# Attention for head pairs on the two halves of the array, with unshifted exponentials, in a kernel of routed attention and a feed-forward

## The chip, the cores and the metric

The kernel runs on one core of a Trainium2 chip, in one launch. The metric is the device time of one execution in microseconds. A core has five engines that are named here as the profile names them: PE (TensorE, with PEld for its weight loads), DVE (VectorE), ACT (ScalarE), POOL (GpSimd) and SP, which issues most transfers.

## The reference

Four batches of eight heads, 768 tokens, 64 numbers per head. Each query and each key is given the nearest of 16 centroids of its head, and a query attends to the keys of its own cluster alone. The result, 3072 tokens of 512 numbers, goes through a feed-forward with a hard-swish between two products.

```python
q_assign = np.argmax(np.einsum('bhsd,hcd->bhsc', q_n, c_n), axis=-1)
k_assign = np.argmax(np.einsum('bhsd,hcd->bhsc', k_n, c_n), axis=-1)
mask = q_assign[:, :, :, None] == k_assign[:, :, None, :]
scores = scale * np.matmul(q, k.transpose(0, 1, 3, 2))
scores = np.where(mask, scores, -1000000000.0)
scores = scores - np.max(scores, axis=-1, keepdims=True)
attn = np.exp(scores)
attn = attn / (np.sum(attn, axis=-1, keepdims=True) + 1e-09)
attn_out = np.matmul(attn, v)          # (B, H, S, D), then x = (B*S, H*D)
h = x @ w_in                           # 512 -> 2048
g = h * np.clip(h + 3.0, 0.0, 6.0) / 6.0
out = g @ w_out                        # 2048 -> 512
```

## The kernel before

All products are in float32 but for the turning of the one-hot clusters. One head is worked at a time (`g` of 32), in six steps of 128 queries (`n` of 192). `xqk` holds per head 80 rows: 64 of q and k with the tokens along the columns (`turn`, L198, on TensorE by way of the identity), and 16 of one-hot clusters (`route`, L212, picks the cluster, `route_turn`, L242, turns the one-hots; those of the keys are -2^60 wherever the cluster is not the key's). One product over the 80 rows thus gives masked scores, 128 queries by 768 keys (`softmax`, L259). VectorE takes the negated maximum (L264), ScalarE the exponentials and their sum (L267), VectorE the reciprocal (L269, L270), GpSimd scales the exponentials (L271). `attn_turn` turns them on TensorE, six blocks per step (L286), and ScalarE and VectorE copy them out of PSUM (L289, L291), half each. After three steps `attn_v` multiplies half a head's values with them, `pv` of 64 rows by 384 queries (L302), and VectorE copies it to `xT` (L306), the input of the feed-forward with its 512 numbers along the rows.

The feed-forward of a batch is a list of 56 items (`ffn_items`): per half sequence 16 upward items of four products with 384 columns (L323), then twelve downward ones of four products with 512 columns (L345). The weights come as float64 bits, 32 chunks, loaded (`load_weights`) and taken apart on VectorE and GpSimd (`decode_weights`), one chunk per step from the first step on.

The order is the program's, moved a little by a scheduler that fills waits. What decides when the feed-forward stands is this:

```python
left = per_batch - (n - 3) % per_batch
for _ in range(-(-len(fill) // left) if n < total else 0):
    fill.pop(0)()
```

The list is filled at the step where `(n - 3) % per_batch` is 47, so `left` is 1 there and all 56 items are issued in that step. What prepares the next head (`prep_items`) lies in the steps of the head before. PSUM pools: `psum_s` two pairs of banks for scores, `psum_t` two banks for everything that is turned, `psum_m` two banks for `pv` and the feed-forward.

Of the kernel before, what the change touches and what calls it, by code (L numbers as in the profile page):

```python
# [19 lines left out]
NCH = S // P  # chunks of 128 tokens in a sequence; chunk j holds the tokens p * NCH + j  # L20
NC2 = 2 * NCH  # q chunks, then k chunks
HALF = S // 2
NHC = NCH // 2
NG = B * H
DM = 512
# [12 lines left out]
@with_exitstack  # L38
def kernel(
    ctx: ExitStack,  # L40
    tc: tile.TileContext,
    q: bass.AP,
    k: bass.AP,
    v: bass.AP,
    centroids: bass.AP,
    moe_w_in: bass.AP,
    moe_w_out: bass.AP,
    out: bass.AP,
):
# [36 lines left out]

    def load(g):
# [9 lines left out]
    # The weights come as the bits of float64: (low, high) words, the high one of sign, 11 exponent  # L97
    # bits and 20 fraction bits. |w| = 2^(e - 1023) (1 + high fraction / 2^20 + low / 2^52), rounded
    # once to float32; the exponent is held to float32's range.

    w_in_v = moe_w_in.bitcast(U32).rearrange("(kt p) (f w) -> kt p f w", p=P, w=2)
    w_out_v = moe_w_out.bitcast(U32).rearrange("(ft p) (m w) -> ft p m w", p=P, w=2)
    chunks = [
        (w_in_sb[:, kt, c * WC : (c + 1) * WC], w_in_v[kt][:, c * WC : (c + 1) * WC])
        for c in range(DFF // WC)
        for kt in range(NKT)
    ] + [(w_out_sb[:, ft], w_out_v[ft]) for ft in range(NFT)]
# [6 lines left out]
    def decode_weights(i):  # L114
        if not 0 <= i < len(chunks):
            return
        dst, raw = chunks[i][0], st.pop(("raw", i))
        lo, hi = raw[:, :, 0], raw[:, :, 1]
        ex = decp.tile([P, WC], U32, name="wex")
        fr = decp.tile([P, WC], U32, name="wfr")  # L120
# [21 lines left out]
        nc.vector.scalar_tensor_tensor(  # L142
            out=dst.bitcast(U32), in0=hi, scalar=0x80000000, in1=fr,
            op0=ALU.bitwise_and, op1=ALU.bitwise_or,
        )

# [1 line left out]

# [294 lines left out]
```

## Time and profile before

| | us |
|---|---|
| median of 3 runs | 1671.39 |
| lowest, highest | 1656.84, 1700.23 |
| span of the profiled execution | 1678.6 |
| TensorE busy in it | 1611.4 |
| VectorE, ScalarE, GpSimd busy | 660.1, 397.7, 254.8 |

The span is counted from the first to the last instruction of the profiled execution. Busy time of TensorE counts each product from its start to its modelled end, and products overlap, so that a mean duration is longer than the spacing of a dense row. The mean granted clock of TensorE over the span is 0.940; its two levels are 1.2 and 2.4 GHz, so 0.5 and 1.0.

### The profile page before, as it was taken

To read this page: it belongs to the slowest core of one execution; us is meant where nothing else is said; L and a number is where in the kernel's file an instruction comes from. 1 tells how busy PE (TensorE), PEld (TensorE's weight loads), DVE (VectorE), ACT (ScalarE), POOL (GpSimd) and SP (SyncE) were. 2 spreads that over 40 slices of the span, in tenths; PEclk is the share of its full clock that TensorE was granted. 3 is DMA by queue.
4 is the path that set the end of the run, shared out by engine and by line. 5 is a ranking of instruction groups with operands and counts; after the bars stand their busy time and mean duration, and the time that the engine had idled before them with its cause. 6 is when DMAs were issued, how large, how long until landed. Compare 5 with 4: busy or idle time off the path is not lost.

```text
span 1678.6 us, 15784 instructions
## 1 busy us (share of the span) xinstructions
PE 1611.4 (96%) x6017; PEld 884.1 (53%) x6017; DVE 660.1 (39%) x1478; ACT 397.7 (24%) x803; POOL 254.8 (15%) x311
## 2 busy tenths in 40 slices
PE   6988889999999999999999999999999999999999
PEld 4544445555545555554545555555554555545453
DVE  5677875411135445520104555341112444542020
ACT  2222233310123333320103333231011333322020
POOL 2445541100001111100001211110000111110000
PEclk9778899999999978999999989799999987999999
DMA  4222321000000000000000000000000000000000
GB/s 129 65 90 89 94 73 29 15 7 12 7 14 28 14 25 19 15 15 13 7 13 21 24 19 19 25 15 4 15 7 13 29 15 5 1 1 1 18 1 19
DMA packets 22107, 42.99 MB, mean 26 GB/s; under 512 B 2576, under 2 KB 14864, under 8 KB 22032
## 3 DMA queue, kind: packets, MB, share of 16 engines
q1 hardware_dynamic: 22032, 41.99, 8.0%
q8 instruction: 48, 0.79, 0.2%
q14 instruction: 27, 0.22, 0.0%
HBM read 35.68 MB, written 6.29 MB: 25 GB/s over the span
## 4 chain that ended last, share of the span: by engine, by line
PE 91%; DVE 4%; POOL 2%; ACT 2%; issue 1%; DMA 0%; SPq 0%; POOLq 0%; ACTq 0%
PE ph L323 20%; PE py L345 20%; PE ps L259 17%; PE pv L302 15%; PE pa L286 9%; PE pr L212 5%; PE pqk L198 2%; PE po L242 2%; ACT pT L289 1%; DVE xqk L203 1%; POOL ex L271 1%; DVE xqk L249 1%; DVE nmx L264 1%; POOL wex L132 0%; ACT ex L267 0%
## 5 line engine op out<-in xcount | busy, mean ns | idle before, releaser
L271 POOL TENSOR_SCALAR ex<-ex,rcp 128x768 f32<-128x768 f32 x192 | 183.4, 957 | 1188.7 <-DVE rcp L270 990.4
L259 PE MATMUL ps<-xqk 80*128 80x384 f32 x768 | 350.3, 569 | 14.0 <-DVE xqk L249 13.1
L323 PE MATMUL ph<-xT,w_in_sb 128*128 128x384 f32 x1024 | 333.0, 487 | 0.0
L345 PE MATMUL py<-w_out_sb,gT 128*128 128x512 f32 x768 | 330.9, 592 | 0.0
L302 PE MATMUL pv<-pT,vt 128*64 128x384 f32 x768 | 285.6, 514 | 0.2 <-ACT pT L289 0.2
L323 PEld LDWEIGHTS ph<-xT,w_in_sb 128*128 128x128 f32 x1024 | 193.9, 190 | 137.5 <-issue 4.9
L345 PEld LDWEIGHTS py<-w_out_sb,gT 128*128 128x128 f32 x768 | 145.9, 190 | 182.0 <-issue 179.9
L289 ACT COPY pT<-pa 128x384 f32<-128x384 f32 x192 | 91.9, 479 | 582.5 <-PE pa L286 581.8
L286 PE MATMUL pa<-ident,ex 128*128 128x128 f32 x1152 | 202.1, 305 | 27.7 <-ACT pT L289 19.9
L286 PEld LDWEIGHTS pa<-ident,ex 128*128 128x128 f32 x1152 | 144.7, 153 | 132.5 <-issue 45.2
L264 DVE TENSOR_REDUCE nmx<-ps 128x1 f32<-128x768 f32 x192 | 183.3, 955 | 77.9 <-PE ps L259 77.2
L267 ACT ACTIVATE ex<-ps,nmx 128x768 f32<-128x768 f32 x192 | 173.1, 902 | 59.8 <-DVE nmx L264 51.2
L259 PEld LDWEIGHTS ps<-xqk 80*128 80x128 f32 x768 | 146.2, 220 | 75.8 <-issue 31.6
L330 ACT ACTIVATE t<-ph,half_c 128x384 f32<-128x384 f32 x128 | 74.4, 581 | 445.1 <-PE ph L323 445.1
L332 DVE SCALAR_TENSOR_TENSOR gT<-t,ph 128x384 f32<-128x384 f32 x128 | 71.0, 555 | 256.9 <-ACT t L330 256.9
L302 PEld LDWEIGHTS pv<-pT,vt 128*64 128x64 f32 x768 | 99.3, 141 | 127.5 <-issue 124.9
L351 DVE COPY y<-py 128x512 f32<-128x512 f32 x24 | 16.6, 692 | 309.2 <-PE py L345 309.2
L291 DVE COPY pT<-pa 128x384 f32<-128x384 f32 x192 | 106.1, 553 | 74.9 <-PE pa L286 74.3
L212 PEld LDWEIGHTS pr<-cnT,xqk 64*128 64x128 f32 x768 | 92.5, 196 | 22.9 <-issue 14.9
L212 PE MATMUL pr<-cnT,xqk 64*128 64x16 f32 x768 | 95.7, 266 | 5.1 <-DVE xqk L203 4.5
L306 DVE COPY xT<-pv 64x384 f32<-64x384 f32 x64 | 35.5, 554 | 150.9 <-PE pv L302 150.7
L198 PE MATMUL pqk<-ident,qk 128*64 128x128 f32 x384 | 63.6, 293 | 0.6 <-ACT xqk L201 0.6
(49 smaller groups left out, 572.3 us busy)
## 6 DMA issues: line engine op xcount, KB each, us to landing
raw<-in_moe_w_in_dram SPq DMA_DIRECT2D x16, 512.0 KB, 3.8
raw<-in_moe_w_out_dram SPq DMA_DIRECT2D x16, 512.0 KB, 3.5
qk<-in_q_dram SPq DMA_DIRECT2D x32, 192.0 KB, 2.4
qk<-in_k_dram SPq DMA_DIRECT2D x32, 192.0 KB, 3.7
vt<-in_v_dram SPq DMA_DIRECT2D x32, 192.0 KB, 2.4
out_dram<-y SPq DMA_DIRECT2D x24, 256.0 KB, 2.0
cen<-in_centroids_dram SPq DMA_DIRECT2D x1, 32.0 KB, 1.8
```

The costliest lines, as they stand in the source:

```text
L198: nc.tensor.transpose(out=pt[:, i], in_=qk[:, j // NCH, j % NCH], identity=ident)
L212: nc.tensor.matmul(pr[:, j], lhsT=xqk[0:D, j], rhs=cnT[:, h * C : (h + 1) * C], start=True, stop=True)
L259: nc.tensor.matmul(sc[:, a], lhsT=xqk[:, i], rhs=xqk[:, NCH + a * NHC : NCH + (a + 1) * NHC], start=True, stop=True,)
L264: nc.vector.tensor_reduce(out=nmx, in_=sc, axis=AX.XY, op=ALU.max, negate=True)
L267: nc.scalar.activation(out=ex, in_=sc, func=ACT.Exp, bias=nmx, scale=1.0, accum_out=den)
L271: nc.gpsimd.tensor_scalar(out=ex, in0=ex, scalar1=rcp, scalar2=1.0, op0=ALU.mult, op1=ALU.mult)
L286: nc.tensor.transpose(out=pt[:, i], in_=ex[:, a, i * P : (i + 1) * P], identity=ident)
L289: nc.scalar.copy(out=dst, in_=pt)
L291: nc.vector.tensor_copy(out=dst, in_=pt)
L302: nc.tensor.matmul(pv[r : r + D, 0:HALF], lhsT=vt[:, j], rhs=pT[:, j], start=(j == 0), stop=(j == NCH - 1),)
L323: nc.tensor.matmul(hh, lhsT=w_in_sb[:, kt, f * P : (f + 1) * P], rhs=xT[:, kt, hf * HALF : (hf + 1) * HALF], start=(kt == 0), stop=(kt == ...
L345: nc.tensor.matmul(py, lhsT=st["g", f][:, i * P : (i + 1) * P], rhs=w_out_sb[:, f], start=(f == 0), stop=(f == NFT - 1),)
```

## The change

The old kernel stays as `general_path`. A new `fast_path` runs first and writes the whole output; a flag that it computes decides whether the old path runs behind it. In the fast path:

- Two heads are worked as a pair (`g` of 16). `turn` turns 128 columns, both heads at once, so that `xf` has the first head in rows 0 to 63 and the second in rows 64 to 127. `route` works on both heads with one product per chunk, against centroids that are zero in the other head's rows. The one-hots lie in `ohs`, zero between the two heads' 16 columns, and are turned to bf16 `xm`.
- `scores` gives keys by queries: 128 keys by 384 queries for each head, f32 over 64 rows, and the mask as a second, bf16 product over 64 rows onto the same PSUM. The exponential is taken without a maximum. `attn_v` uses the exponentials as they are, the two heads to the two halves of the columns of `pv`. No exponential is turned.
- GpSimd adds up the exponentials over the key chunks (`acc`), and `divide` sums them over the rows with a product against ones (`pd`), takes reciprocals on VectorE, and multiplies. There VectorE and GpSimd also keep track of sums and reciprocals for the flag.
- The feed-forward items are spread: `left` is 48 at the step that fills the list, and the number of items is rounded down. 32 weight chunks are taken in 60 steps.
- `psum_t` has one buffer, `psum_v` is new, `qkp` has one buffer. `decode_chunk`, `weight_chunks` and `unit_rows` hold the old code of weights and centroids as functions.

```diff
...
+def fast_path(ctx, tc, ok, q, k, v, centroids, moe_w_in, moe_w_out, out):
...
+    qkp = pool("qkp", 1)
+    vp = pool("vp", 2)
+    xp = pool("xp", 2)
...
+    expp = pool("expp", 4)
+    accp = pool("accp", 2)
+    nump = pool("nump", 2)
...
+    psum_s = pool("psum_s", 2, space=PSUM)
+    psum_v = pool("psum_v", 1, space=PSUM)
+    psum_t = pool("psum_t", 1, space=PSUM)
+    psum_m = pool("psum_m", 2, space=PSUM)
...
+    ones = const.tile([P, D], F32, name="ones")
...
+    ohs = [const.tile([P, NC2, P], BF16, name=f"oh{i}") for i in range(2)]
+    good = const.tile([P, HALF], F32, name="good")
+    inverses = const.tile([P, HALF], F32, name="inverses")
...
+    def turn(g, part):
+        if part == 0:
+            st["xf", g] = xp.tile([P, NC2, P], F32, name="xf")
+        qk, xf = st["qk", g], st["xf", g]
+        pt = psum_t.tile([P, NHC, P], F32, name="pqk", tag="t")
+        for i in range(NHC):
+            j = part * NHC + i
+            nc.tensor.transpose(out=pt[:, i], in_=qk[:, j // NCH, j % NCH], identity=ident)
...
+    def route(g):
+        c0, xf = (2 * g) % H * C, st["xf", g]
+        pr = psum_t.tile([P, NC2, 2, C], F32, name="pr", tag="t")
+        for j in range(NC2):
+            nc.tensor.matmul(
+                pr[:, j], lhsT=xf[:, j], rhs=cnT[:, c0 : c0 + 2 * C], start=True, stop=True
+            )
+        shape = [P, 2 * NC2, C]
+        pr = pr.rearrange("p j t c -> p (j t) c")
+        mx = rtp.tile([P, 2 * NC2], F32, name="mx")
...
+        oh = ohs[g % 2].rearrange("p j (t c) -> p j t c", t=2)
+        tie = tie.rearrange("p (j t) c -> p j t c", t=2)
+        first = first.rearrange("p (j t) -> p j t", t=2)
+        for a, op in ((0, ALU.is_equal), (1, ALU.not_equal)):
+            sl = slice(a * NCH, (a + 1) * NCH)
+            nc.vector.tensor_tensor(
+                out=oh[:, sl, :, 0:C], in0=tie[:, sl],
+                in1=first[:, sl].unsqueeze(3).to_broadcast([P, NCH, 2, C]), op=op,
+            )
...
+    def route_turn(g, part):
+        if part == 0:
+            st["xm", g] = xp.tile([P, NC2, P], BF16, name="xm")
+        xm = st["xm", g]
+        po = psum_t.tile([P, 4, P], F32, name="po", tag="t")
+        for i in range(4):
+            j = part * 4 + i
+            nc.tensor.matmul(
+                po[:, i], lhsT=ohs[g % 2][:, j], rhs=(ident_q if j < NCH else ident_k),
+                start=True, stop=True,
+            )
...
+    def scores(n):
+        g, hf, j = where(n)
+        xf, xm = st["xf", g], st["xm", g]
+        qs = slice(hf * NHC, (hf + 1) * NHC)
+        ps = psum_s.tile([P, 2, 512], F32, name="ps")
+        sc = ps[:, :, 0:HALF]
+        for x, first in ((xf, True), (xm, False)):
+            for t in range(2):
+                r = slice(t * D, (t + 1) * D)
+                nc.tensor.matmul(
+                    sc[:, t], lhsT=x[r, NCH + j], rhs=x[r, qs], start=first, stop=not first
+                )
+        ex = expp.tile([P, 2, HALF], F32, name="ex")
+        nc.scalar.activation(out=ex, in_=sc, func=ACT.Exp, scale=SM_SCALE)
+        st["ex", n] = ex
+        if j == 1:
+            acc = st["acc", g, hf] = accp.tile([P, 2, HALF], F32, name="acc")
+            nc.gpsimd.tensor_tensor(out=acc, in0=st["ex", n - 1], in1=ex, op=ALU.add)
+        elif j > 1:
+            acc = st["acc", g, hf]
+            nc.gpsimd.tensor_tensor(out=acc, in0=acc, in1=ex, op=ALU.add)
+        if hf == 1 and j == NCH - 1:
+            st.pop(("xf", g)), st.pop(("xm", g))
+
+    def attn_v(n):
+        g, hf, j = where(n)
+        if j == 0:
+            st["pv"] = psum_v.tile([P, 512], F32, name="pv")
+        pv, vt, ex = st["pv"][:, 0:HALF], st["v", g], st.pop(("ex", n))
+        for t in range(2):
+            nc.tensor.matmul(
+                pv[t * D : (t + 1) * D], lhsT=vt[:, j, t], rhs=ex[:, t],
+                start=(j == 0), stop=(j == NCH - 1),
+            )
+        if j == NCH - 1:
+            num = st["num", g, hf] = nump.tile([P, HALF], F32, name="num")
+            nc.scalar.copy(out=num, in_=pv)
+            if hf == 1:
+                st.pop(("v", g))
+
+    def divide(n):
+        g, hf, _ = where(n)
+        b, kt = divmod(g, NKT)
+        if kt == 0 and hf == 0:
+            st["xT", b] = xtp.tile([P, NKT, S], F32, name="xT")
+        acc, num = st.pop(("acc", g, hf)), st.pop(("num", g, hf))
+        pd = psum_t.tile([P, 512], F32, name="pd", tag="t")
+        pd = pd[:, 0:HALF]
+        for t in range(2):
+            nc.tensor.matmul(
+                pd[t * D : (t + 1) * D], lhsT=ones, rhs=acc[:, t], start=True, stop=True
+            )
+        rcp = nump.tile([P, HALF], F32, name="rcp")
+        nc.vector.reciprocal(out=rcp, in_=pd)
+        nc.vector.tensor_tensor(
+            out=st["xT", b][:, kt, hf * HALF : (hf + 1) * HALF], in0=num, in1=rcp, op=ALU.mult
+        )
+
+        nc.vector.scalar_tensor_tensor(
+            out=good, in0=pd, scalar=BOUND, in1=good, op0=ALU.is_le, op1=ALU.mult
+        )
+        nc.gpsimd.tensor_tensor(out=inverses, in0=inverses, in1=rcp, op=ALU.add)
...
+    def prep_items(g):
+
+        return {
+            0: lambda: turn(g, 0),
+            1: lambda: turn(g, 1),
+            2: lambda: turn(g, 2),
+            3: lambda: turn(g, 3),
+            5: lambda: route(g),
+            7: lambda: route_turn(g, 0),
+            8: lambda: route_turn(g, 1),
+            9: lambda: route_turn(g, 2),
+        }
+
+    fill = []
+    per_pair = 2 * NCH
+    per_batch = NKT * per_pair
+    total = NPAIR * per_pair
...
+    lag_v, lag_d = 2, 4
+    for n in range(total + lag_d):
+        g, r = divmod(n, per_pair)
+        if n < total:
+            if r == 4:
+                load(g + 2, "q", "k")
+                load(g + 1, "v")
+            scores(n)
+        if lag_v <= n < total + lag_v:
+            attn_v(n - lag_v)
+        m = n - lag_d
+        if m >= 0 and m % NCH == NCH - 1:
+            divide(m)
+            if m % per_batch == per_batch - 1:
+                fill += ffn_items(m // per_batch)
+
+        for i in range(n * 8 // 15, (n + 1) * 8 // 15):
+            decode_weights(i - 1)
+            load_weights(i)
+        if g + 1 < NPAIR and r in (items := prep_items(g + 1)):
+            items[r]()
+        left = per_batch - (m + 1) % per_batch
+        for _ in range(len(fill) // left if n < total else 0):
+            fill.pop(0)()
+    for it in fill:
+        it()
+
+    low = smallp.tile([P, 1], F32, name="low")
+    nc.vector.scalar_tensor_tensor(
+        out=good, in0=inverses, scalar=BOUND, in1=good, op0=ALU.is_le, op1=ALU.mult
+    )
+    nc.vector.tensor_reduce(out=low, in_=good, axis=AX.X, op=ALU.min)
+    pl = psum_t.tile([1, P], F32, name="pl", tag="t")
+    nc.tensor.transpose(out=pl, in_=low, identity=ident)
+    every = smallp.tile([1, 1], F32, name="every")
+    nc.vector.tensor_reduce(out=every, in_=pl, axis=AX.X, op=ALU.min)
+    nc.vector.tensor_copy(out=ok, in_=every)
...
+def general_path(ctx, tc, q, k, v, centroids, moe_w_in, moe_w_out, out):
...
+    ins = (q, k, v, centroids, moe_w_in, moe_w_out)
+    flagp = ctx.enter_context(tc.tile_pool(name="flagp", bufs=1))
+    ok = flagp.tile([1, 1], I32, name="ok")
+    with ExitStack() as inner:
+        fast_path(inner, tc, ok, *ins, out)
+    with tc.If(tc.nc.values_load(ok[0:1, 0:1], min_val=0, max_val=1) == 0):
+        with ExitStack() as inner:
+            general_path(inner, tc, *ins, out)
...
```

The order of TensorE's instructions at the end of the first batch, before: one turn of exponentials, the last values of the batch, and the whole feed-forward behind it (L286 turns, L302 values, L323 and L345 feed-forward, L212 routing, L259 scores).

```order
L286 MATMUL pa<-ident,ex 128x128 x6
L302 MATMUL pv<-pT,vt 64x384 x6
L323 MATMUL ph<-xT,w_in_sb 128x384
L212 MATMUL pr<-cnT,xqk 128x16 x12
L323 MATMUL ph<-xT,w_in_sb 128x384 x63
L345 MATMUL py<-w_out_sb,gT 128x512 x48
L323 MATMUL ph<-xT,w_in_sb 128x384 x64
L345 MATMUL py<-w_out_sb,gT 128x512 x48
L259 MATMUL ps<-xqk 128x384 x2
```

The same engine in the changed kernel, a step of the second batch: scores (L300) of both heads, the mask of both, values (L321) of both, one feed-forward item (L368), and the next step.

```order
L300 MATMUL ps<-xf 128x384 x2
L300 LDWEIGHTS xm
L300 MATMUL ps<-xm 128x384
L300 LDWEIGHTS xm
L300 MATMUL ps<-xm 128x384
L321 MATMUL pv<-ex,vt 64x384 x2
L368 MATMUL ph<-xT,w_in_sb 128x384 x4
L300 MATMUL ps<-xf 128x384 x2
```

The feed-forward moved from one block behind the attention to four products behind each step, and the turns of the exponentials are gone.

TensorE in the changed kernel where a division falls into the same step as a turn of the next pair: `pd` (L342) and the turn `pqk` (L228) use the one buffer of `psum_t`.

```order
L321 MATMUL pv<-ex,vt 64x384 x2
L342 MATMUL pd<-acc,ones 64x384 x2
L368 MATMUL ph<-xT,w_in_sb 128x384 x4
L300 MATMUL ps<-xf 128x384
L228 MATMUL pqk<-ident,qk 128x128 x3
L300 MATMUL ps<-xf 128x384
L300 LDWEIGHTS xm
```

Between `pd` and the turn stand one feed-forward item and the first head's scores; in the kernel before no product of this kind stands.

VectorE in the changed kernel, first batch: the division (L346, L352, L347) between the steps that take weights apart (L57 to L77) and the mask's copy (L284).

```order
L77 SCALAR_TENSOR_TENSOR w_in_sb<-raw,wfr 128x512
L346 RECIPROCAL rcp<-pd 128x384
L352 SCALAR_TENSOR_TENSOR good<-pd,good 128x384
L347 TENSOR_TENSOR xT<-num,rcp 128x384
L57 TENSOR_SCALAR wex<-raw 128x512
L61 TENSOR_SCALAR wfr<-raw 128x512
L284 CAST xm<-po 128x512
```

The reciprocal of 128 by 384 sums and the flag's test come ahead of the multiplication, and the mask's copy behind them; before, the reciprocals were of one column.

## Rows read from the trace of the kernel before

**Rows 1.** The page, busy time of the engines over the whole span.

```profile
PE 1611.4 (96%) x6017; PEld 884.1 (53%) x6017; DVE 660.1 (39%) x1478; ACT 397.7 (24%) x803; POOL 254.8 (15%) x311
```

**Rows 2.** Stretches: length; busy PE, PEld, DVE, ACT, POOL; granted clock; DMA share.

```profile
26.00:315.80 289.80, 261.40 (x1082) 146.12 (x1080) 203.66 (x447) 85.74 (x177) 120.16 (x140) 0.86 0.23 70
315.80:483.40 167.60, 167.60 (x473) 87.69 (x473) 23.89 (x46) 18.59 (x32) 0.91 (x1) 1.00 0.03 9
483.40:718.10 234.70, 228.48 (x1034) 130.45 (x1032) 119.62 (x280) 79.89 (x168) 42.57 (x47) 0.91 0.07 21
...
1282.40:1507.40 225.00, 216.91 (x951) 122.29 (x949) 110.87 (x260) 74.19 (x156) 40.76 (x45) 0.89 0.04 11
1507.40:1674.90 167.50, 167.48 (x455) 85.67 (x454) 21.76 (x38) 18.62 (x32) 0.00 (x0) 1.00 0.02 8
```

**Rows 3.** Groups by line and form, TensorE: busy us, mean ns; idle before.

```profile
L259 PE MATMUL ps<-xqk 80*128 80x384 f32 x768 | 350.3, 569 | 14.0 <-DVE xqk L249 13.1 <-ACT ex L267 0.8
...
L323 PE MATMUL ph<-xT,w_in_sb 128*128 128x384 f32 x1024 | 333.0, 487 | 0.0
...
L345 PE MATMUL py<-w_out_sb,gT 128*128 128x512 f32 x768 | 330.9, 592 | 0.0
...
L302 PE MATMUL pv<-pT,vt 128*64 128x384 f32 x768 | 285.6, 514 | 0.2 <-ACT pT L289 0.2
...
L286 PE MATMUL pa<-ident,ex 128*128 128x128 f32 x1152 | 202.1, 305 | 27.7 <-ACT pT L289 19.9 <-POOL ex L271 3.8 <-ACT xqk L247 2.3
...
L212 PE MATMUL pr<-cnT,xqk 64*128 64x16 f32 x768 | 95.7, 266 | 5.1 <-DVE xqk L203 4.5 <-ACT pT L289 0.6
...
L242 PE MATMUL po<-ident_k,oh 128*16 128x128 bf16 x192 | 23.1, 232 | 4.2 <-ACT pT L289 3.5 <-ACT xqk L247 0.7
```

**Rows 4.** Timeline of TensorE around one change from column to row half.

```profile
1011.42 0.39 PE L242 MATMUL po<-ident_k,oh 128*16 128x128 bf16 x4
...
1020.19 0.19 PEld L302 LDWEIGHTS pv<-pT,vt 128*64 128x64 f32 x2 [0.17 <-issue]
...
1020.19 4.08 PE L302 MATMUL pv<-pT,vt 128*64 128x384 f32 x12
...
1020.57 0.14 PEld L302 LDWEIGHTS pv<-pT,vt 128*64 128x64 f32 x1 [0.18 <-issue]
...
1020.89 0.14 PEld L302 LDWEIGHTS pv<-pT,vt 128*64 128x64 f32 x1 [0.19 <-issue]
...
1023.47 0.14 PEld L302 LDWEIGHTS pv<-pT,vt 128*64 128x64 f32 x1 [0.19 <-issue]
...
1024.20 2.75 PEld L212 LDWEIGHTS pr<-cnT,xqk 64*128 64x128 f32 x24 [0.60 <-issue]
...
1024.20 2.85 PE L212 MATMUL pr<-cnT,xqk 64*128 64x16 f32 x24
```

**Rows 5.** Pieces of the chain that ended last: start us, us, what.

```profile
26.02 5.12 PE ps L259 x8
...
1510.37 40.83 PE ph L323 x126
1551.20 41.20 PE py L345 x96
```

**Rows 6.** Groups by line and form, the other engines.

```profile
L271 POOL TENSOR_SCALAR ex<-ex,rcp 128x768 f32<-128x768 f32 x192 | 183.4, 957 | 1188.7 <-DVE rcp L270 990.4 <-PE pqk L198 124.2 <-DVE rcp L269 36.4
...
L267 ACT ACTIVATE ex<-ps,nmx 128x768 f32<-128x768 f32 x192 | 173.1, 902 | 59.8 <-DVE nmx L264 51.2 <-DVE rcp L270 5.1 <-DVE rcp L269 2.9
...
L291 DVE COPY pT<-pa 128x384 f32<-128x384 f32 x192 | 106.1, 553 | 74.9 <-PE pa L286 74.3
...
L270 DVE RECIPROCAL rcp<-rcp 128x1 f32<-128x1 f32 x192 | 30.0, 156 | 2.5
...
L269 DVE TENSOR_SCALAR rcp<-den 128x1 f32<-128x1 f32 x192 | 28.1, 146 | 32.0 <-ACT ex L267 31.2
```

More of the change, by code (lines that the diff above doesn't have):

```diff
@@ L24 @@
 NG = B * H
+NPAIR = NG // 2
 DM = 512
@@ L35, with weight_chunks @@
 FAR = 2.0**60
[L38 to L49, printed above, removed]
+BOUND = 2.0**60
+def weight_chunks(w_in_sb, w_out_sb, moe_w_in, moe_w_out):
+    w_in_v = moe_w_in.bitcast(U32).rearrange("(kt p) (f w) -> kt p f w", p=P, w=2)
+    w_out_v = moe_w_out.bitcast(U32).rearrange("(ft p) (m w) -> ft p m w", p=P, w=2)
+    return [
+        (w_in_sb[:, kt, c * WC : (c + 1) * WC], w_in_v[kt][:, c * WC : (c + 1) * WC])
+        for c in range(DFF // WC)
+        for kt in range(NKT)
+    ] + [(w_out_sb[:, ft], w_out_v[ft]) for ft in range(NFT)]
@@ new lines, in unit_rows @@
+def unit_rows(nc, smallp, cen, n):
+    sq = smallp.tile([P, n], F32, name="censq")
+    ss = smallp.tile([P, 1], F32, name="censs")
+    nc.vector.tensor_tensor(out=sq, in0=cen, in1=cen, op=ALU.mult)
+    nc.vector.reduce_sum(out=ss, in_=sq, axis=AX.X)
+    low = smallp.tile([P, 1], F32, name="cenlow")
+    nc.vector.tensor_scalar_max(out=low, in0=ss, scalar1=1e-30)
+    nrm = smallp.tile([P, 1], F32, name="cennrm", tag="cennrm")
+    nc.scalar.sqrt(nrm, low)
+    for it in range(2):
+        rr = smallp.tile([P, 1], F32, name="cenrr", tag="cenrr")
+        nc.vector.reciprocal(out=rr, in_=nrm)
+        two = smallp.tile([P, 1], F32, name="centwo", tag="centwo")
+        nc.vector.scalar_tensor_tensor(
+            out=two, in0=ss, scalar=rr, in1=nrm, op0=ALU.mult, op1=ALU.add
+        )
+        nrm = smallp.tile([P, 1], F32, name="cennrm", tag="cennrm")
+        nc.vector.tensor_scalar(
+            out=nrm, in0=two, scalar1=0.5, scalar2=(1e-6 if it else 0.0), op0=ALU.mult, op1=ALU.add
+        )
+    rden = smallp.tile([P, 1], F32, name="cenrden")
+    nc.vector.reciprocal(out=rden, in_=nrm)
+    cn = smallp.tile([P, n], F32, name="cencn")
+    nc.vector.tensor_scalar_mul(out=cn, in0=cen, scalar1=rden)
+    return cn
@@ L95, in load @@
         st["qk", g], st["v", g] = qk, vt
[L101 to L107, printed above, removed]
+    chunks = weight_chunks(w_in_sb, w_out_sb, moe_w_in, moe_w_out)
     def load_weights(i):
@@ L114, in decode_weights @@
     def decode_weights(i):
[L115 to L120, printed above, removed]
[L121 to L145 removed]
+        if 0 <= i < len(chunks):
+            decode_chunk(nc, decp, chunks[i][0], st.pop(("raw", i)))
     def constants():
@@ L157, in centroid_norm @@
     def centroid_norm(cen):
[L158 to L181 removed]
+        cn = unit_rows(nc, smallp, cen, D)
         pc = psum_t.tile([D, P], F32, name="pc", tag="t")
@@ L410, with kernel @@
         it()
+@with_exitstack
+def kernel(
+    ctx: ExitStack,
+    tc: tile.TileContext,
+    q: bass.AP,
+    k: bass.AP,
+    v: bass.AP,
+    centroids: bass.AP,
+    moe_w_in: bass.AP,
+    moe_w_out: bass.AP,
+    out: bass.AP,
+):
+    ins = (q, k, v, centroids, moe_w_in, moe_w_out)
[6 more added lines that the diff above has]
+            general_path(inner, tc, *ins, out)
 _INS = ["q", "k", "v", "centroids", "moe_w_in", "moe_w_out"]
```

214 lines of the change are left out of this document (170 added, 44 removed).

## The prediction

> **What bounds the kernel now.** I read the page's busy time first, then the stretches, then single lines. TensorE is busy for 1611 of 1679 us and no other engine passes 40% [rows 1], so the end moves only with TensorE's work, its clock and its gaps. The stretches show four attention blocks with a feed-forward block behind each [rows 2]: attention takes 290 us for the first batch and 235 to 225 us for the others, a feed-forward 167.6 us, and 26 us pass ahead of the first scores [rows 5]. In a feed-forward block TensorE is never idle and the clock is granted whole; in attention it is granted 0.86 to 0.91. An attention step is one of 192 (128 queries of one head before, 128 keys by 384 queries of two heads after).
>
> Busy time per line overlaps, so I price by spacing. The chain has 126 passes of 384 columns in 40.83 us, 0.32 each, and 96 of 512 columns in 41.20, 0.43 each; at half clock a 384-column pass takes 0.64 [rows 5]. An f32 product is two passes (768 in the row of L259, for 384 products) [rows 3]. A pass that only has 128 weight columns to load comes every 0.12 us (24 in 2.85) [rows 4]. Four bf16 products of 128 columns end in 0.39, one lasts 0.23, so each further one is 0.053 [rows 3, 4].
>
> A change of array shape costs too. The last weights of the values' product load at 1023.47; by the even 0.32 its pass starts at 1023.79 and leaves at 1024.11, but the next shape's weights load only at 1024.20 [rows 4]. That is 0.09 lost, and the first weights are not loaded ahead: 0.38 instead of 0.32 to the next load for 64 columns, 0.12 for 128. So 0.15 into the column halves, 0.20 elsewhere.
>
> As a test: an attention step at full clock now holds 4 passes of scores and 4 of values (2.56), 6 turns (0.72), 4 of routing (0.48), 2 of q and k (0.24), 2 one-hots (0.12) and some 0.17 of shape changes, 4.3 us. The first batch takes 290/48 = 6.0 (1.4 times that), the others 4.7 to 4.9 (1.1 times): half clock and waits are the rest.
>
> **The change, part by part.** *Removed:* 1152 turns of the exponentials, 1152 x 0.12 = 138 us of TensorE; the maximum, the scaling and the turned copies on the other engines lay beside it and are worth nothing by themselves. *Halved:* turns of q and k to 192 (23 us), routing to 384 passes (46), one-hot turns to 192 with 128 weight columns, priced at 0.12 like the other loads (23; the bf16 row gives 10).
>
> *Same count, other place:* scores and values keep 768 passes each, but two heads sit on two halves. No row shows two halves at work at once. The bounds are no overlap (spacing 0.32 as in every row) and full overlap (half). Program order puts both passes of one head next to each other. In the rows weights are loaded one pass ahead at most, and passes start in order [rows 4]. If that holds, the second pass of the first head waits for its own half, the first pass of the second head starts beside it, and the rest follows: three slots of 0.32 instead of four. I take this, since it is what the start order of the rows gives; the ends stay as rivals. The Trainium skill, TensorE: Matmul & The Clock Gate, Part 3 "Packing small matmuls", says that products on different tiles run side by side with starts some 4 ns apart, and that products start and end strictly in program order; the second half of this speaks against a full gain here, the first half against none.
>
> *Added:* the mask, two bf16 passes of 384 columns per step, 0.16 each from the bf16 row (0.32 if priced as f32; I take 0.16, the same type); 128 passes of `pd`, 41 us; and shape changes, now three per step: scores (row half), values (column half), feed-forward (whole), 0.20 + 0.15 + 0.20 = 0.55.
>
> Per step, in us:
> - Scores and mask 4 x 0.32 + 2 x 0.16 = 1.60 one after the other; 1.12 with the overlap above (3.5 slots of 0.32); 0.80 in full.
> - Values 1.28, 0.96 or 0.64.
> - Small products (23 + 46 + 23 + 41)/192 = 0.69; 0.64 and 0.58 with `pd` overlapped.
> - Shape changes 0.55.
> - Together 4.12, **3.27** or 2.57.
>
> *Feed-forward moved.* Its work stays (167.6 per batch), but one item now stands behind each step instead of a block. This hides the exponentials and copies: a mixed step is 3.27 + 503/140 = 6.9 us, while ACT has an exponential of 0.9 [rows 6] and some copies, and GpSimd one addition. So I price mixed steps at TensorE's own work, at full clock: half of each is what now runs at 1.00 [rows 2].
>
> *First batch.* Without feed-forward the other engines come close. Decoding costs VectorE (203.7 - 119.6)/32 = 2.6 us per chunk and GpSimd (120.2 - 42.6)/32 = 2.4, first against second attention block [rows 2]; at 8 chunks in 15 steps 1.4 and 1.3 per step. GpSimd's sum of exponentials has two inputs; the row with one is 0.96 for the same size [rows 6], twice that is the upper bound, 1.9, which I take. Five sums in six steps make 1.6, in all 3.0 per step. VectorE has per pair copies, routing and masks of about 5.4 (ten of the 0.55 kind [rows 6]) and two divisions of 5.1 (below), 1.3 per step, 2.7 in all. TensorE has two shape changes here, 3.07, and I apply the first batch's 1.4: 4.3 us. It stays the bound. 48 steps and 4 of lag make 52 x 4.3 = 223 us.
>
> *One buffer for turns.* `psum_t` has one buffer, and `pd` uses it. The next turn must wait until VectorE has taken the reciprocal and the test on it. RECIPROCAL of one column takes 156 ns, another operation on one column 146 [rows 6]: 10 ns per element makes 384 x 10 + 150 = 4.0 us. A copy of that size takes 0.55, the lower bound; I take 4.0, since it is the only row of this operation. The Trainium skill, VectorE: DVE Perf Modes, "First, the fixed hardware budget", gives the reciprocal a repeat count of 8 per element; an estimate from that is 384 x 8 / 0.96 GHz = 3.2 us, by which the stall here would be 19 us less in the whole sum. `pd` is free 0.3 + 4.0 + 0.6 = 4.9 us after its products; a feed-forward item (2.6 or more) and half of the next scores (0.7) stand between, 3.3. TensorE, with all behind it, stalls 1.6 us, 24 times in the mixed stretches: 38 us (0 with the short reciprocal). The 8 of the first batch lie in its factor.
>
> *Free:* loads (as many bytes; DMA share 0.23 at most [rows 2]; the single `qk` buffer is refilled one step after its last turn, eight steps ahead of its next use; SP waits there for that turn, and only weight chunks, one in two steps, are queued behind), the eight centroid loads and longer constants (beside the first loads; 5 us if not). Flag and branch at the end: 4 us with the last copy, unknown, 0 to 10.
>
> **Sum against the profiled execution:** 26 start + 223 first batch + 140 x 3.27 = 458 attention of the other batches + 503 three feed-forwards + 38 stalls + 168 last feed-forward + 5 end = 1421 us. The profiled run's 1679 lies 7 us above the median of 1671, so 1414.
>
> **Rivals.**
> 1. *The halves don't overlap* (the change doesn't do what its name says): 52 x (3.92 x 1.4) = 285, 140 x 4.12 = 577, rest as above: 1602, less 7, 1595. For it: every row has passes one by one. Against it: nothing in the rows has tried two halves.
> 2. *They overlap in full:* 180 (3.3 per step, where GpSimd's 3.0 is near) + 360 + stalls of 45 because the cover is shorter: 1287, less 7, 1280. For it: only one head's weights need to stay in each half, so nothing but the order of the passes stands against it. The Trainium skill, on the page and in the part named above, gives a measured speedup of 3.07 for four packed tiles. Against it: two passes of the same half stand next to each other, and the rows keep starts in order.
> 3. *Slower: half clock.* Attention stretches were granted 0.86 to 0.91, feed-forward ones 1.00 [rows 2]. If half-filled arrays brought 1.2 GHz wherever attention runs, its 192 x 3.27 = 628 us would double: 64 of that is already in the first batch's factor, so 1421 + 564 = 1985, less 7, 1978. It turns into a loss from some 257 us on, 40% of the attention at 1.2 GHz. Against it: half of each mixed step is the work that holds 1.00 now.
> 4. *First batch bound by GpSimd or VectorE,* which delay each other's decoding: 5.5 us per step, 286 instead of 223, 1477.
> 5. *The test fails and the old path runs too,* about 1650 us more. In these inputs each cluster holds 26 to 72 keys of its head and scores are under 0.06, so every sum lies near 26 to 72, far inside the bounds.
>
> **How the numbers follow.** Three slots of four 0.46, full 0.26, none 0.20, first batch 0.03, half clock 0.04, old path 0.01. The predicted time is the first's, 1414. Its own spread is 70 either way (stall 0 to 40, first-batch factor 1.1 to 1.6, mask at 0.32 adds 50). The range reaches from a little under the full case to just over the middle of the serial one, 1265 to 1600; outside lie the upper serial cases, half clock and old path. A change within 2% (some 33 us, about what this kernel's runs of 1657 to 1700 can tell from none) needs the serial case plus a slow first batch: 0.06. Slower takes half clock or the old path: 0.05. Faster 0.89.
>
> **What would show it.** Starts of the score passes: pairs at the same moment mean overlap; even gaps of 0.32 mean none. The second stretch on: 6.9 us per mixed step and clock 1.00. RECIPROCAL near 4 us, and turns (L228, L276) waiting for VectorE at L352. A first batch of 220 us, GpSimd under 3.0 per step. Wrong would be the whole sum if feed-forward rows show idle TensorE, or granted clock under 0.9 beyond the first batch.

## The result, and the profile after

The changed kernel takes **1273.5 us** (median; 1272.5 to 1276.9) against 1671.3 us for the kernel before on the same chip: a ratio of **0.763, interval 0.758 to 0.767**. That is inside the predicted range, 141 us under the predicted 1414, and half a per cent from rival 2 (full overlap, 1280), whose terms did not all hold, as told below. Ratios leave out executions more than 1.5% above the fastest of their kernel; the profile of the first experiment is of such a longer one.

First the page of the changed kernel: busy time of the engines, and the granted clock in 40 slices. They answer to [rows 1].

```profile
PE 1196.9 (94%) x4610; PEld 546.9 (43%) x4610; DVE 439.0 (34%) x588; ACT 270.3 (21%) x403; POOL 409.5 (32%) x315
...
PEclk9788878799999999999999999999999999999999
```

TensorE has a quarter fewer instructions and 414 us less busy time, a little more than the 404 us between the two spans. GpSimd is the one engine with more to do. The clock is lower in slices 2 to 8, the first batch, and 0.9 or more from there on.

The stretches of the changed kernel answer to [rows 2] (length; busy PE, PEld, DVE, ACT, POOL; granted clock; DMA share). The cuts are the first scores (17.2), the first feed-forward product (237.5), two free points, the point a feed-forward's length ahead of the end (1099; the last attention product starts at 1080) and the last product (1266.4).

```profile
17.20:237.50 220.30, 163.79 (x782) 67.75 (x782) 174.75 (x211) 54.06 (x76) 158.03 (x132) 0.83 0.33 92
237.50:500.00 262.50, 262.50 (x1051) 121.26 (x1050) 81.82 (x111) 62.76 (x94) 83.04 (x55) 0.98 0.10 25
500.00:780.00 280.00, 280.00 (x1120) 127.88 (x1119) 74.19 (x101) 66.17 (x99) 78.40 (x47) 0.99 0.09 22
780.00:1099.00 319.00, 319.00 (x1197) 141.74 (x1196) 76.08 (x99) 66.74 (x99) 82.96 (x50) 0.99 0.06 16
1099.00:1266.40 167.40, 167.40 (x455) 86.04 (x454) 21.89 (x38) 18.59 (x32) 0.00 (x0) 1.00 0.03 10
```

From 237.5 to 1266.4 TensorE is not idle for a moment. The three rows from 237.5 to 1099, 861.5 us, hold 140 steps and three feed-forwards and are called the mixed stretch below; less 503 us for these, a step costs 358.5/140 = **2.56 us**. The same 140 steps plus four cost 1507.4 - 315.8 - 503 = 689 us before [rows 2], 4.8 each. By stretch the 404 us are: 330 from those steps, 70 from the first batch (290 to 220), 9 from an earlier start (26 to 17.2), none from the last feed-forward, and 4 lost at the end, where the flag is read (3.7 to 8.1 us behind the last product).

A timeline of one mixed step, TensorE only (start, length, operation), answers to [rows 4]:

```profile
602.49 0.92 PE L300 MATMUL ps<-xf 64*128 64x384 f32 x4
603.24 0.33 PE L300 MATMUL ps<-xm 64*128 64x384 bf16 x2
603.50 0.87 PE L321 MATMUL pv<-ex,vt 128*64 128x384 f32 x4
604.30 0.30 PE L242 MATMUL pr<-cnT,xf 128*128 128x32 f32 x1
```

Four score passes and two masks take 603.50 - 602.49 = 1.01 us, four passes of values 0.80. With the shape changes of 0.20 and 0.15 taken off, 0.81 and 0.65 are left, the "full" bounds of 0.80 and 0.64. The pairs show in short windows of the same timeline, each of which prints what runs in it (602.490 to 602.498, 602.6 to 602.9, 603.25 to 603.45):

```profile
602.49 0.59 PE L300 MATMUL ps<-xf 64*128 64x384 f32 x1
...
602.49 0.59 PE L300 MATMUL ps<-xf 64*128 64x384 f32 x2
...
602.92 0.49 PE L300 MATMUL ps<-xf 64*128 64x384 f32 x2
```

One pass at 602.49, two before 602.6, two more from 602.92: the records' starts are 602.494, 602.500, 602.920 and 602.927. The first passes of both heads start 6 ns apart, then both second passes 7 ns apart, although the program has both passes of the first head ahead of the second head's. Passes of one half never come that close (0.43 and 0.32 in the second experiment), so each pair is one pass of either half. In 13 of the 140 mixed steps a turn (of q and k, or of one-hots) stands between the two heads' scores, and these don't pair.

### The profile page after: what moved, and what is told of

Same layout as the page of the kernel before. It is cut to its first block, busy times and chain, and to the rows that moved or that the text cites. A ratio compares the mean times of both kernels' runs of the same rounds, so it can differ in the third digit from the quotient of the medians.

```text
span 1274.5 us, 11438 instructions
## 1 busy us (share of the span) xinstructions
PE 1196.9 (94%) x4610; PEld 546.9 (43%) x4610; DVE 439.0 (34%) x588; ACT 270.3 (21%) x403; POOL 409.5 (32%) x315
## 4 chain that ended last, share of the span: by engine, by line
PE 82%; DVE 8%; POOL 6%; issue 2%; DMA 1%; ACTq 0%; ACT 0%; POOLq 0%
PE ph L368 27%; PE py L390 27%; PE ps L300 12%; PE pv L321 9%; DVE wfr L76 3%; PE pr L242 3%; POOL acc L311 2%; PE pqk L228 2%; POOL wex L64 1%; PE pd L342 1%; POOL wfr L70 1%; POOL wex L67 1%; PE po L276 1%; DVE wfr L73 1%; DVE rcp L346 1%
## 5 line engine op out<-in xcount | busy, mean ns | idle before, releaser
L368 PE MATMUL ph<-xT,w_in_sb 128*128 128x384 f32 x1024 | 359.3, 501 | 0.0
L311 POOL TENSOR_TENSOR acc<-acc,ex 128x768 f32<-128x768 f32 x128 | 241.0, 1883 | 327.5 <-ACT ex L304 325.9
L304 ACT ACTIVATE ex<-ps 128x768 f32<-128x768 f32 x192 | 155.7, 811 | 463.9 <-PE ps L300 455.4
L368 PEld LDWEIGHTS ph<-xT,w_in_sb 128*128 128x128 f32 x1024 | 190.9, 193 | 146.9 <-issue 25.3
L300 PE MATMUL ps<-xf 64*128 64x384 f32 x768 | 201.1, 569 | 0.0
L321 PE MATMUL pv<-ex,vt 128*64 128x384 f32 x768 | 176.9, 541 | 0.0
L308 POOL TENSOR_TENSOR acc<-ex 128x768 f32<-128x768 f32 x32 | 58.8, 1839 | 234.4 <-ACT ex L304 234.0
L300 PEld LDWEIGHTS ps<-xf 64*128 64x128 f32 x768 | 66.1, 197 | 109.5 <-issue 99.8
L346 DVE RECIPROCAL rcp<-pd 128x384 f32<-128x384 f32 x32 | 81.8, 2555 | 72.6 <-PE pd L342 72.6
L321 PEld LDWEIGHTS pv<-ex,vt 128*64 128x64 f32 x768 | 39.6, 140 | 95.4 <-issue 86.8
L300 PE MATMUL ps<-xm 64*128 64x384 bf16 x384 | 70.6, 341 | 0.0
L76 DVE TENSOR_TENSOR wfr<-wfr,wex 128x512 f32<-128x512 f32 x32 | 50.2, 1570 | 1.5 <-POOL wex L67 1.0
L242 PE MATMUL pr<-cnT,xf 128*128 128x32 f32 x384 | 48.4, 285 | 0.0
```

The costliest lines, as they stand in the source:

```text
L76: nc.vector.tensor_tensor(out=fr_f, in0=fr_f, in1=ex_f, op=ALU.mult)
L242: nc.tensor.matmul(pr[:, j], lhsT=xf[:, j], rhs=cnT[:, c0 : c0 + 2 * C], start=True, stop=True)
L300: nc.tensor.matmul(sc[:, t], lhsT=x[r, NCH + j], rhs=x[r, qs], start=first, stop=not first)
L304: nc.scalar.activation(out=ex, in_=sc, func=ACT.Exp, scale=SM_SCALE)
L308: nc.gpsimd.tensor_tensor(out=acc, in0=st["ex", n - 1], in1=ex, op=ALU.add)
L311: nc.gpsimd.tensor_tensor(out=acc, in0=acc, in1=ex, op=ALU.add)
```

## The experiments

Ratios are to the kernel before on the chip of that run (1672, 1679 and 1680 us); the changed kernel is at 0.763, beside 1671 us. It was not run again beside these, so a difference of a few us from its 1273.5 may be the chip's.

**Both heads' scores on one half of the rows.** The second head's scores come from the first head's rows of `xf` and `xm`, so its output is another.

```diff
-                r = slice(t * D, (t + 1) * D)
+                r = slice(0, D)
```

> The second head's scores and mask are taken from the first head's rows, so that all score passes lie on the same row half; passes, weight loads and order are those of the changed kernel (the second head's output is then not its own). Theory A (the two halves work at the same time, worth 0.80 us of scores and mask per step): the 140 steps beside the feed-forward grow by 0.80 us each, 112 us; the first batch, where TensorE was busy for 164 of 220 us, by 0 to 38. In all 1385 us (1380 to 1425), and the score passes show spacings of 0.32 instead of pairs. Theory B (overlap is worth little, the gain came from the turns that are gone and from the feed-forward standing behind each step): under 1300 us.

Measured: 0.859 (0.854 to 0.865), some 160 us more than the changed kernel and above the expected range. The first batch and the mixed stretch:

```profile
18.30:313.50 295.20, 287.02 (x783) 124.59 (x782) 148.83 (x211) 54.76 (x76) 151.02 (x132) 0.81 0.24 69
313.50:1276.50 963.00, 963.00 (x3363) 448.83 (x3363) 231.66 (x312) 195.78 (x292) 244.88 (x152) 0.99 0.07 19
```

The mixed stretch is 963 us instead of 861.5, so 101.5/140 = 0.72 us per step against 0.80 expected of full overlap and 0.48 of three slots; the 13 steps without pairs have nothing to lose here, and 0.80 x 127/140 is 0.73. The other 59 of the 160 us then lie in the first batch, for which at most 38 were expected; in this longer execution it takes 295 us instead of 220, with a granted clock of 0.54 from 200 to 300 us.

**Scores and values on one half.** As above, and both heads' values go to the lower half of `pv`, as one sum; the other half of the result is set to 1.

```diff
-                pv[t * D : (t + 1) * D], lhsT=vt[:, j, t], rhs=ex[:, t],
-                start=(j == 0), stop=(j == NCH - 1),
+                pv[0:D], lhsT=vt[:, j, t], rhs=ex[:, t],
+                start=(j == 0 and t == 0), stop=(j == NCH - 1 and t == 1),
...
```

> As the run before, and the values of both heads also go to the same column half (their sums are added up in one place, the other half is filled with ones; the output is not the reference's). Theory A: 0.80 + 0.64 = 1.44 us per step, 202 us in 140 steps, and 0 to 69 us in the first batch, so 1475 to 1545 us. Theory B: under 1330 us.

Measured: 0.912 (0.908 to 0.916), 1522 us. The first batch and the mixed stretch:

```profile
17.40:299.80 282.40, 261.27 (x785) 114.49 (x783) 181.07 (x225) 54.79 (x76) 167.94 (x149) 0.87 0.27 76
299.80:1345.20 1045.40, 1045.40 (x3363) 483.95 (x3363) 222.59 (x298) 196.97 (x292) 246.20 (x166) 1.00 0.06 16
```

The mixed stretch is 184 us longer than in the changed kernel, 1.31 us per step, and the first batch 62. The timeline of this kernel, and last the short window 640.1 to 640.3:

```profile
640.06 1.55 PE L300 MATMUL ps<-xf 64*128 64x384 f32 x4
641.45 0.48 PE L300 MATMUL ps<-xm 64*128 64x384 bf16 x2
641.87 1.50 PE L321 MATMUL pv<-ex,vt 128*64 128x384 f32 x4
...
640.06 0.59 PE L300 MATMUL ps<-xf 64*128 64x384 f32 x1
```

The same six passes that took 1.01 us take 1.81 here (640.06 to 641.87), and one pass runs where two ran. One pass follows the other by 0.43 us, then by 0.32. So the two halves are worth 249 us of the 398 (62 of them in the first batch, where waits and the clock have a part), and all else in the change 149. Without any overlap the kernel would still be ahead of the one before, and below rival 1's 1595.

**Another order of the passes.** All of one head's scores stand ahead of the other head's, the mask too.

```diff
-        for x, first in ((xf, True), (xm, False)):
-            for t in range(2):
+        for t in range(2):
+            for x, first in ((xf, True), (xm, False)):
```

> Program order of a step's scores by head instead of by product: first head f32, first head mask, second head f32, second head mask. If each half takes its own passes from a queue of its own (theory C), pairs start together as before and the time stays at 1274 us, within 6. If it is neighbours in the program that run together, as the prediction took it (theory D), only the first head's mask meets the second head's first pass: a step's scores take 1.44 instead of 0.80 us, 140 x 0.64 = 90 us more, 1345 to 1385.

Measured: 0.766 (0.763 to 0.769), 1278.9 us. Short windows of its timeline (642.17 to 642.19, 642.3 to 642.6, 642.95 to 643.1):

```profile
642.18 0.59 PE L300 MATMUL ps<-xf 64*128 64x384 f32 x1
...
642.18 0.60 PE L300 MATMUL ps<-xf 64*128 64x384 f32 x2
...
642.61 0.49 PE L300 MATMUL ps<-xf 64*128 64x384 f32 x2
642.93 0.33 PE L300 MATMUL ps<-xm 64*128 64x384 bf16 x2
```

The program now has three passes of one head in a row, yet the second head's first pass starts with the first one's, and the first head's mask, which stands ahead of it in the program, starts 0.74 us after it (642.934 and 642.194). Each half takes its next pass when it is free, whatever stands between in the program.

**The feed-forward in one block again.** The items are handed out in the step that fills the list. To have the weights in time, decoding is denser.

```diff
-        for i in range(n * 8 // 15, (n + 1) * 8 // 15):
+        for i in range(n * 2 // 3, (n + 1) * 2 // 3):
...
-        left = per_batch - (m + 1) % per_batch
-        for _ in range(len(fill) // left if n < total else 0):
+        left = per_batch - m % per_batch
+        for _ in range(-(-len(fill) // left) if n < total else 0):
```

> The feed-forward of a batch stands in one block behind its attention, as in the kernel before, instead of one item behind each step; since its weights are then needed earlier, 2 chunks in 3 steps are taken apart instead of 8 in 15. Theory A: attention steps alone still hold some 2.4 us of TensorE, above ACT (0.8) and POOL (1.7), and lose as in the kernel before by half clock and waits a tenth to a fifth: 25 to 70 us, and up to 45 us for the denser decoding in the first batch; 1300 to 1390 us. Theory B (the spreading is the larger part of the gain): above 1450 us.

Measured: 0.768 (0.765 to 0.771), 1281.1 us: only 7.5 more, where 1300 to 1390 was expected. Stretches: the first batch, an attention block between two feed-forwards, and that block's feed-forward; then TensorE's waits from 249.1 to 1103.5 us (us, times, longest).

```profile
17.20:249.10 231.90, 170.18 (x783) 72.39 (x781) 181.23 (x216) 54.16 (x76) 160.26 (x134) 0.81 0.33 90
...
420.60:542.10 121.50, 117.92 (x698) 49.78 (x696) 51.02 (x62) 46.61 (x66) 77.74 (x46) 0.97 0.15 35
542.10:707.00 164.90, 164.90 (x452) 85.21 (x451) 25.15 (x40) 19.07 (x33) 2.46 (x2) 1.00 0.04 13
```

```profile
PE pqk L228 <- DVE good L352: 5.8, 9, 1.2
PE po L276 <- DVE good L352: 5.4, 11, 0.5
```

Turns do wait on `psum_t` for VectorE at L352 where no feed-forward covers it, 20 times, but only 0.56 us each, 11 in all. A block has fewer shape changes (387 against 450 in TensorE's records of this stretch), and from the first feed-forward to the end of attention this kernel takes 854 us against 861.5. Its loss lies in the first batch (232 against 220 us), where the decoding is denser. Spreading is worth next to nothing here.

**The kernel before with its feed-forward spread.** The list is emptied over 48 steps, and `pv` takes the pool of the turns.

```diff
-        pv = psum_m.tile([P, 512], F32, name="pv", tag="m")
+        pv = psum_t.tile([P, 512], F32, name="pv", tag="t")
...
-        left = per_batch - (n - 3) % per_batch
-        for _ in range(-(-len(fill) // left) if n < total else 0):
+        left = per_batch - (n - 2) % per_batch
+        for _ in range(len(fill) // left if n < total else 0):
```

> The kernel before with its feed-forward spread over the next batch's steps as in the changed kernel (and pv moved to the pool of the turns, so that an open sum of the feed-forward doesn't hold its bank). Theory A: what attention loses alone (4.7 to 4.9 us per step against 4.3 by its passes, granted clock 0.91) goes away when each step has feed-forward behind it: 140 x 0.4 = 60 us less, 1590 to 1640 us. Theory B (as with the changed kernel, where a block cost 8 us): within 20 us of 1671.

Measured: 0.970 (0.967 to 0.974), 50 us less. In two of its mixed stretches TensorE is never idle, with a clock of 0.97 to 0.98 (0.96 in the one ahead of them), where attention alone was granted 0.86 to 0.91 in [rows 2] and 0.93 in the block that these leave out (885.7 to 1114.8 us):

```profile
900.00:1200.00 300.00, 300.00 (x1195) 169.12 (x1194) 117.96 (x261) 81.77 (x163) 34.45 (x38) 0.98 0.05 16
1200.00:1450.00 250.00, 250.00 (x931) 134.51 (x930) 87.79 (x194) 59.29 (x120) 27.20 (x30) 0.97 0.03 9
```

The same spreading is worth 50 us to the old attention and 7.5 at most to the new: the parts of this change don't add up.

**Fewer sums on GpSimd.** Of five additions of exponentials per half pair only the first is left, so the denominators lack four chunks.

```diff
-        elif j > 1:
-            acc = st["acc", g, hf]
-            nc.gpsimd.tensor_tensor(out=acc, in0=acc, in1=ex, op=ALU.add)
```

> GpSimd adds only the first two chunks of exponentials of each half head pair, 32 additions instead of 160; the sums and the output are then not the reference's. Theory P (the first batch is bound by VectorE and GpSimd, which slow each other: L76 takes 0.69 alone and up to 2.3 us, mean 1.57): L76 falls under 0.9 on average and the first batch from 220 to 150 to 180 us, 1200 to 1235 us in all. Theory Q (the first batch is TensorE's, with its clock at 0.83): over 1255 us.

Measured: 0.741 (0.738 to 0.744), 1243.6 us. One group by line of the changed kernel, and then the same line of this one (busy, mean ns):

```profile
L76 DVE TENSOR_TENSOR wfr<-wfr,wex 128x512 f32<-128x512 f32 x32 | 50.2, 1570 | 1.5 <-POOL wex L67 1.0
```

```profile
L76 DVE TENSOR_TENSOR wfr<-wfr,wex 128x512 f32<-128x512 f32 x32 | 24.2, 756 | 0.9 <-POOL wex L67 0.5
```

VectorE's own work is the same, and its two-input addition halves when GpSimd's go. The first batch falls from 220 to 187.5 us, which is the whole gain of 30; expected were 150 to 180:

```profile
18.00:205.50 187.50, 148.76 (x782) 63.52 (x781) 144.03 (x211) 54.00 (x76) 89.73 (x98) 0.93 0.39 108
```

Of these 33 us, 18 are idle time of TensorE (56.5 us in the changed kernel, 38.7 here) and 15 busy time for the same 782 records, with a granted clock of 0.93 instead of 0.83. The run takes away GpSimd's own time (158 to 90 us) together with its effect on VectorE, so it doesn't tell the two apart, and why the clock is higher was not tried.

**Weights decoded later.** Two kernels spread the 32 chunks over more steps in the program (from step 48 on at 4 in 5, or at 6 in 5).

```diff
-        for i in range(n * 8 // 15, (n + 1) * 8 // 15):
+        when = lambda n: n // 3 if n < 48 else 16 + (n - 48) * 4 // 5
+        for i in range(when(n), when(n + 1)):
```

> Weights are taken apart later: 16 chunks in the first 48 steps instead of 26, the other 16 in the 20 steps behind. Theory P: ten chunks less in the first batch, each with some 4.5 us on VectorE and 2.3 on GpSimd there, 25 to 45 us less, 1228 to 1250 us, and nothing lost behind it, where VectorE is busy for 30%. Theory Q: 1265 to 1275 us.

> The same with 8 chunks in the first 48 steps and 24 in the 20 steps behind. Theory P: a further 8 chunks, down to what TensorE needs in the first batch (52 steps of 2.4 us at full clock, 125 us; at 0.83 150): 1195 to 1235 us, if no feed-forward product waits for its weights. Theory Q: 1265 to 1275 us.

Measured: 0.761 and 0.758, the changed kernel's time. Inconclusive: the scheduler moved the decoding ahead again, 28 and 27 of 32 chunks inside the first batch as before.

**Weights held back.** The same two schedules, and a copy on ScalarE from that step's exponentials into the load's buffer, so that the load can't start earlier.

```diff
+            nc.scalar.copy(out=raw[:, 0:1, 0:1].bitcast(F32), in_=st["ex", n][:, 0:1, 0:1])
             nc.sync.dma_start(st["raw", i], chunks[i][1])
...
```

> The weights are really taken apart later: each chunk's buffer is first touched by a copy of one column of that step's exponentials on ScalarE, so that neither its load nor its decoding can be moved ahead; 16 chunks in the first 48 steps. (With the program order alone the scheduler moved them ahead again: 28 chunks ran before 230 us in the two runs that tried it, as in the changed kernel.) Theory P (the first batch of 220 us is bound by VectorE and GpSimd): ten chunks less at some 4 us of VectorE each, down to the 188 us that the first batch took with few sums: 1235 to 1255 us. Theory Q: over 1265 us.

> The same with 8 chunks in the first 48 steps and 24 in the next 20. Theory P: TensorE becomes the bound of the first batch, at 52 steps of 2.4 us and a granted clock of 0.8 to 0.9 150 to 185 us instead of 220; 1205 to 1245 us, if the feed-forward doesn't wait for weights. Theory Q: over 1265 us.

Measured: 0.756 (0.753 to 0.758) and 0.763 (0.760 to 0.766), 3 us less and 10 more. The first batch does fall, to 197 and 184.5 us (granted clock 0.91 and 0.90), but the mixed stretch grows by 18 and 43. The stretch from 250 to 300 us in the changed kernel, in the first of these and in the second:

```profile
250.00:300.00 50.00, 50.00 (x213) 24.48 (x213) 20.18 (x30) 14.42 (x22) 17.56 (x12) 0.97 0.05 12
```

```profile
250.00:300.00 50.00, 40.77 (x155) 18.30 (x152) 36.82 (x49) 12.24 (x24) 31.43 (x29) 0.88 0.25 70
```

```profile
250.00:300.00 50.00, 34.52 (x125) 15.49 (x125) 40.12 (x52) 9.89 (x22) 31.44 (x32) 0.83 0.31 92
```

With the decoding VectorE is busy for 37 to 40 us of 50 there, TensorE idles for 9 to 15, and its clock is lower, although feed-forward products stand beside it. That these would cover the decoding was wrong.

**Two steps at a time.** Scores of two steps, values of two, then the other work of both, so that the array's shape changes half as often in the program's order, apart from what the scheduler moves.

```diff
-    for n in range(total + lag_d):
+    for n0 in range(0, total + lag_d, 2):
+        for n in (n0, n0 + 1):
             ...
             scores(n)
+        for n in (n0, n0 + 1):
             attn_v(n - lag_v)
+        for n in (n0, n0 + 1):
             ...
```

> Two attention steps at a time: scores of both, then values of both, then two feed-forward items, so that array shapes change three times in two steps instead of three times in one. Theory S (a shape change costs TensorE 0.15 to 0.20 us, three a step are 0.55 of the 2.56 us that a step takes beside its feed-forward): 140 x 0.27 = 38 us less behind the first batch and 0 to 9 in it, 1225 to 1240 us. Rival T (the time goes into waits for exponentials instead, which are now needed sooner): 1260 us or more, with TensorE idle behind the first batch.

Measured: 0.738 (0.736 to 0.741), 1240.4 us, 33 less. The mixed stretch is 44 us shorter, 0.31 us per step, against the 0.55/2 = 0.27 that halving the prediction's shape changes gives:

```profile
244.10:1061.70 817.60, 814.96 (x3368) 394.26 (x3367) 233.72 (x315) 194.79 (x292) 244.94 (x152) 1.00 0.08 22
```

But they are not halved: TensorE's records change shape 288 times here and 450 times in the changed kernel's mixed stretch. The 162 fewer are worth 30 us at the prediction's 0.15 to 0.20 each. The rest is an estimate from the rows: 11 us from the clock (1.00 instead of 0.98 to 0.99) and some 7 because only 4 steps don't pair instead of 13, less 3 for new waits.

**Both: two steps at a time and the weights held back** (the first schedule).

> Two steps at a time and 16 gated chunks in the first 48 steps, together. If S and P hold and are independent, their savings add up: 1190 to 1225 us. If the first batch's bound is TensorE at half clock, two steps at a time may lengthen its waits, and the sum falls short: 1225 to 1245.

Measured: 0.727 (0.725 to 0.730), **1223.3 us**, the best of all and 50 under the changed kernel. Here holding the weights back gives 17 us on top, where alone it gave 3 against the changed kernel, which was not run beside it. In the profiled executions the first batch falls by 34 us and the mixed stretch grows by 25, 9 less together; alone it was 23 and 18, 5 less. Whether it gives more beside two steps than alone is not shown.

## Why the prediction was right and wrong, point by point

- **Scores and values, the step that failed.** "*three slots of 0.32 instead of four. I take this, since it is what the start order of the rows gives*". Those rows show passes in order because every product there follows another on the same rows and columns; they hold no case of two halves, and I carried their order over. Measured are two slots: 2.56 us per step against the 2.57 of the full case and the 3.27 taken, which over 140 steps is 99 of the 141 us. The pairs of starts and the reordered kernel show the mechanism, the kernels on one half its price: 0.72 for the scores (0.80 in the sum), 1.31 - 0.72 = 0.59 for the values (0.64).
- **The page against the trace.** The Trainium skill, TensorE: Matmul & The Clock Gate, Part 3 "Packing small matmuls", says that products on different tiles start some 4 ns apart; the trace is near that, with 6 to 10 ns. It also says that products start strictly in program order; across two halves the trace does not agree: the first head's mask starts 0.74 us after a product that stands behind it in the program.
- **One buffer for turns.** 38 us predicted, none measured in the mixed stretches. RECIPROCAL was mis-sized:

```profile
L346 DVE RECIPROCAL rcp<-pd 128x384 f32<-128x384 f32 x32 | 81.8, 2555 | 72.6 <-PE pd L342 72.6
L311 POOL TENSOR_TENSOR acc<-acc,ex 128x768 f32<-128x768 f32 x128 | 241.0, 1883 | 327.5 <-ACT ex L304 325.9
```

  2.55 us instead of 4.0 (these groups are of the changed kernel). The 10 ns per element was the difference of two durations of one column each, another operation's for the fixed part, and such a difference carries no slope. `pd` is then free after 0.3 + 2.6 + 0.6 = 3.5 us, with a cover of 3.3 by the prediction's count; even with the feed-forward in one block the turns waited 0.56 us each time, not 1.6. GpSimd's addition, taken at 1.9, is 1.88.
- **First batch: right size, wrong reason.** 223 predicted, 220 measured, and rival 4 ("delay each other") at 286 was meant to be another case. But TensorE's own work there is less than was assumed (busy for 163.8 of 220.3 us, at a granted clock of 0.83), and the chain of waits between 60 and 140 us is VectorE's and GpSimd's, in turns:

```profile
63.36 1.12 POOL wex L64
64.56 0.95 POOL wfr L70
65.53 0.69 DVE wfr L73
66.28 0.88 issue
67.16 2.31 DVE wfr L76
69.49 2.17 DVE w_in_sb L77
71.67 2.47 DVE rcp L346
```

  The run with fewer sums shows that GpSimd's additions lengthen VectorE's decoding. So rival 4's mechanism was there, at 220/52 = 4.2 us per step instead of 5.5; how much of it is VectorE slowed down, GpSimd's own time or the clock, no run tells apart. The factor of 1.4 came from a first batch whose waits were others; that it hit is luck.
- **Feed-forward moved.** "*This hides the exponentials and copies*": TensorE indeed never idles, but in a block the new attention hardly idles either (3.6 of 121.5 us), so it hid little. The kernel before had more to gain from it (50 us).
- **Shape changes.** The sum has three per step; the trace has 450 in 140 steps, 3.2. Their price of 0.15 to 0.20 fits the timeline above and explains 30 of the 44 us that two steps at a time save; that run doesn't halve them, so its 0.31 us per step is no measure of the 0.55.
- **Clock.** Full beyond the first batch (0.98 to 1.00), and 0.97 with attention in a block of its own, so half-filled arrays did not bring 1.2 GHz (rival 3). Which part of the old attention held its clock at 0.86 to 0.93 was not tried. The row from which the prediction took 0.64 us for a pass at half clock (26.02 us in [rows 5]) lies in a stretch whose granted clock is given as 1.00; the same 0.64 is found from 80 to 88 us, where it is 0.50.
- **Start and end.** 17.2 instead of 26, and 8 instead of 5: 4.4 us more than the 3.7 before, where the flag is read and the branch taken, and the sum had left 1. The old path did not run (rival 5).

Together: 99 for the overlap, 38 for the stall, 9 for the start and 3 for the first batch, less 3 at the end, make 146; the spans' offset to the median, taken as 7 and measured as 1, takes 6 back: 140 of the 141 us. Rival 2's 1280 is nearer, but not in all its terms: its first batch of 180 (its own 52 x 3.3 is 172) was 220, its start of 26 was 17, and its stalls of 45 were none.

## What to carry to other kernels

Before taking an order of starts from a trace, look whether any row in it holds the case that you carry it to; rows of one array shape say nothing about two halves, and a bound that no row excludes deserves its share of the forecast. Small products on halves of the array are worth pairing, and same-shaped ones worth grouping: pairing was worth 249 us here and grouping 33 more. Where other engines slow each other down, moving their work beside TensorE's does not make it free: what two delayed schedules of decoding saved in the first batch came back behind it, most of it for one and more than all for the other.

## What the runs showed of the hardware that was not expected

- The two halves of the array behave as if each had a queue of its own: a product starts 0.74 us ahead of one that precedes it in the program, when that one waits for its own half.
- A VectorE addition of 128x512 with two inputs (L76, L141 before) takes 709 ns in the kernel before, 1570 beside GpSimd's additions, up to 2.31 us in the chain above, and 756 when four of five of these are gone. The Trainium skill, GPSIMD Engine Reference, section 8 "Key points", says that the two share their SBUF interfaces and contend where a VectorE instruction has two SBUF inputs; the trace agrees, with 1570 ns for 709:

```profile
L141 DVE TENSOR_TENSOR wfr<-wfr,wex 128x512 f32<-128x512 f32 x32 | 22.7, 709 | 2.9 <-POOL wex L132 2.3
```

- RECIPROCAL of 128x384 takes 2.55 us, 4.6 times a copy of that size (0.555).
